# Token rows scattered to their pages in DRAM, in place of lists and row fetches

## The chip, the core and the metric

The kernel runs on one core of a Trainium2 chip. The metric is device time in microseconds (us) of one execution; the median of several runs is given. Engines are named as in the profile: PE (TensorE), with its weight loads PEld; DVE (VectorE); ACT (ScalarE); POOL (GpSimd); SP (SyncE, which here only issues DMAs and loads a register).

## What is computed

A long convolution over four sequences, gated by its own input, and then a mixture of 16 experts of which each token takes one:

```
h_filt = (maximum(pos_emb @ w1, 0) @ w2) * exp(-0.01 * pos)      # 10048 x 128
u = x * v                                                        # 4 x 10048 x 128
y = irfft(rfft(u, 2 * S) * rfft(h_filt, 2 * S))[:S]              # along the sequence
x = (x * y).reshape(40192, 128)

g_idx = argmax(x @ w_group)            # one of 4 groups, g_w its softmax weight
e_idx = argmax(x @ w_expert[g_idx])    # one of 4 experts in it, e_w its softmax weight
out[token] = g_w * e_w * (maximum(x[token] @ moe_w1[g, e], 0) @ moe_w2[g, e])   # 128 -> 1024 -> 128
```

All inputs and outputs are fp32. The expert products are made of fp32r halves: a high part (`wh`, `xh`, `hh`) and the rest (`wl`, `xl`, `hl`), three matmuls for each product.

## The kernel before

**Convolution.** The transform is a two-stage DFT. After the filter's own transform, a loop runs over b = 0..4. For b = 0..3 its first part transforms batch b: 42 parts of three channels each, whose inputs `xv` arrive by SP (L364) and are folded into even and odd halves `eo` (L380 add, L381 subtract; on POOL for batch 0 and for the first 12 parts of batches 2 and 3, on DVE otherwise), then multiplied on PE (`dft_blocks`, L320). From b = 1 on, the inverse of batch b-1 runs in the same loop: small PE transposes of `z` (`turned`, L583 and L593), `inverse_blocks` (L624), and a product with the gate `x` (L637). I call this the DFT stage of batch b. Its second part is the middle of batch b: 40 pairs of positions, each with a load `ht` (L540), two products on DVE (`t`, L551 and L554), two sums on POOL (`y`, L552 and L555) and the inverse's first product on PE. For b = 4 there is only the inverse of batch 3: the last stage.

**Routing.** A finished batch's rows `xy` are written to DRAM (`xyd`, L696). In the next middle and the DFT stage after it, the generators `chosen` and `ranked` find each token's expert, weight and place, step by step between the other work. Places are counted so that each expert's tokens fill pages of 256 rows. `ranked` then hands out 79 scatters per batch: each is one indirect DMA of POOL (L855) that writes 128 entries of 8 bytes (token number and weight) to their places in a DRAM array `list`. The program calls `scatter(3)` after each part of a DFT stage and `scatter(1)` in each pair of a middle. On POOL a scatter is held only behind the last sum `y` that was written before it (`mark`, `behind`), and the builder's scheduler places it after that.

**Experts.** 164 pages of 256 rows follow. `load_list` (L1053) loads the lists of 16 to 70 pages at once. For each page two indirect DMAs of POOL gather 2 x 128 rows of 512 bytes (`xg`, L1136, six buffers), PE transposes them (`px`, L1151), 48 matmuls make the two layers (L1189 to L1191 and L1208 to L1210), ACT scales the rows (`os`, L1229), and two indirect DMAs of POOL write them out by token (`out`, L1234, queued up to 24 pages deep). `turn` fixes the order of PE, DVE and ACT for each page over its neighbours; `fetch` sets what POOL gets in each page: two gathers first, then scatters that are still owed, then writes as far as a budget of 4.8 operations (`SHARE`) reaches. A page's second-layer weights come by SP (`ws`, L1129). Of the four differences `wl` (L1178) of a page three are made on DVE; the fourth, of the second half of `ws`, is made on POOL for pages 8 to 41 (`FROM, TO`) and on DVE for the others.

`beyond` and `between` fix POOL's order in the last part: an instruction put `between` comes after the last `beyond` before it in the program and before the next one.

Of the kernel before, what the change touches and what calls it, by code (L numbers as in the profile page):

```python
# [32 lines left out]
TP = 256  # L33
# [7 lines left out]
FROM, TO = 8, 42  # L41
XG, OS = 6, 24
SHARE = 4.8
EARLY = 16
LISTED = 3
# [9 lines left out]
NLOAD, NPROD, NSPEC, NTT, NY = 5, 5, 5, 5, 5  # L55
BIGID = 65535.0
HALVES = slice(0, 64), slice(64, 128)
# [73 lines left out]
class Kernel:  # L131
# [5 lines left out]
    def emit(self):  # L137
        tc, nc, d = self.tc, self.nc, self.d
        with ExitStack() as ctx:
# [14 lines left out]
            self.entries = ctx.enter_context(tc.tile_pool(name="entries", bufs=2))  # L154
            self.all = [Page(self, q) for q in range(pg.n)]
            self.lists = st
# [11 lines left out]
    def router_consts(self):  # L168
# [7 lines left out]
        self.keep = rp.tile([128, 8, NB], mybir.dt.bfloat16, name="keep")  # L176
# [4 lines left out]
        self.iota = rp.tile([128, 2], F32, name="iota")  # L181
# [6 lines left out]
    def conv(self, ctx, right):  # L188
# [23 lines left out]
        routing, self.scatters, self.mark = iter(()), [], None  # L212

        self.anchor, self.loose = None, []
        for b in range(self.nbat + 1):
# [13 lines left out]
            for j, (d0, n) in enumerate(groups(120, GI) + [(120, 4), (124, 4)]):  # L229
                if b > 0 and j % 2 == 0:  # L230
                    tts = self.turned(d0, min(2 * GI, D - d0))
                for i in range(2 * j, min(2 * j + 2, len(parts))):
                    self.run_ahead(b, i, made, folded)
                    self.dft_blocks(*folded[i])
                    if b > 0 and i % 2 == 0:
                        self.inverse_blocks(b - 1, xy, d0, n, tts)
                if last:
                    self.inverse_blocks(b - 1, xy, d0, n, tts)
                    next(weights, None)
                    if j == 1:  # L240
                        for p in self.all[:XG]:
                            p.gather()
# [11 lines left out]
            if not last:  # L254
                back = []
                for i, (k0, n) in enumerate(groups(NB, 2)):
# [3 lines left out]
                    final = b == self.nbat - 1  # L260
                    self.scatter(i > 3 and (i < 22 or not final))
                    if final and i == 22:
                        self.scatter(NB)
                        ready = self.load_list(0, nc.gpsimd)
                    if final and i == 26:
                        ready(nc.gpsimd)
# [13 lines left out]
    def behind(self, ins):  # L280

        if self.mark is not None:
            order = mybir.DependencyInfo(mybir.DependencyClass.NoSync, mybir.DependencyReason.DATA)
            self.tc.add_manual_dep(ins.ins, self.mark.ins.name, order, reason="in its turn")

# [4 lines left out]
    def between(self, ins):  # L290

        self.tc.keep_in_program_order(ins)
        self.after(ins, self.anchor)
# [9 lines left out]
    def scatter(self, n):  # L303
        for _ in range(n):
            if self.scatters:
                ins = self.scatters.pop(0)()
                if self.anchor is not None:
                    self.between(ins)
                else:
                    self.behind(ins)  # L310
# [35 lines left out]
    def product(self, b, d0, n):  # L346
# [3 lines left out]
        if b == 0 and d0 >= FIRST:  # L350
# [6 lines left out]
            tag, bufs = ("spec", NSPEC) if d0 // GD % 9 < 5 else ("tt", NTT)  # L357
# [12 lines left out]
    def fold(self, xt, b, d0, n):  # L370
# [8 lines left out]
        sub = nc.vector if (b or d0 >= FIRST and odd) and not early else nc.gpsimd  # L379
        self.in_turn(b, add.tensor_tensor(eo[:, :n, 0:64], lo, hi, ALU.add))  # L380
        self.in_turn(b, sub.tensor_tensor(eo[:, :n, 64:128], lo, hi, ALU.subtract))  # L381
# [31 lines left out]
    def network(self, ctx, eo):  # L413
# [6 lines left out]
        w1, w2 = tp.tile([128, 128], F32, name="w1f"), tp.tile([128, 256], F32, name="w2f")  # L420
# [40 lines left out]
    def filter(self, ctx, ahead, made, folded):  # L461
# [12 lines left out]

        ent = fp.tile([128, self.pages.nt, 2], F32, name="ent")
        nc.gpsimd.memset(ent[:, :, 0], BIGID)
        nc.gpsimd.memset(ent[:, :, 1], 0.0)
        nc.gpsimd.dma_start(d["list"].rearrange("(p t) c -> p t c", p=128), ent)
# [56 lines left out]
    def middle(self, b, k0, n):  # L535
# [19 lines left out]
        self.mark = nc.gpsimd.tensor_tensor(y[:, :n, 1], t1[:, :n, 1], t1[:, :n, 0], ALU.subtract)  # L555
# [43 lines left out]
    def inverse_blocks(self, b, xy, d0, n, tts):  # L599
# [37 lines left out]
        nc.vector.tensor_tensor(  # L637
            xy[:, :, d0 : d0 + n].rearrange("p t d -> p d t"), yt[:, :n], xo[:, :n], ALU.mult
        )

# [45 lines left out]
    def chosen(self, b, xy, oh, en):  # L686
# [6 lines left out]
        for u in range(len(units) + 2):  # L693
# [23 lines left out]
            if u > 1:  # L717
# [9 lines left out]
                if o + n == NCH or t0 + n == NB:  # L727
                    n, t0 = o + n, t0 - o
                    lg = rp.tile([128, NCH, 20], F32, tag="lg", name="lg", bufs=2)[:, :n]
# [12 lines left out]
    def ranked(self, b, oh, en):  # L742
# [55 lines left out]
        v.tensor_tensor(base, base, self.rem, ALU.subtract)  # L798
        yield
# [12 lines left out]
        for h in range(2):  # L812
# [518 lines left out]
```

## Time and profile before

| | us |
|---|---|
| median of 3 runs (lowest to highest) | 2476.6 (2474.68 to 2480.05) |
| the profiled execution's own time | 2463.86 |
| span of the profiled execution, first to last instruction | 2462.1 |
| PE busy | 2040.5 (83%) |
| DVE busy | 1744.9 (71%) |
| ACT busy | 1366.1 (55%) |
| POOL busy | 1468.6 (60%) |
| first page's `xh` to the last page's | 1238.2 to 2437.2 |

The 40 slices of the page show PE near full with three gaps, at about 500 to 570, 810 to 890 and 1090 to 1170 us. A row of a group reads: line, engine, operation, output<-input, count | busy us, mean ns of one | idle time before it and its releasers. A row of the windows gives, for a stretch of the span, each engine's busy us, and at its end the granted PE clock, the DMA engines' busy share and GB/s. A row of the timeline gives start, duration, engine, line and what was idle before it, with the releaser; "issue" is idle time in which the profile shows nothing waited for.

### The profile page before, as it was taken

The page shows a single profiled execution, that of the slowest core. Times are in us where ns is not written, and L with a number is a line of the kernel's source. Part 1 is how long each engine was busy: PE and PEld are TensorE (multiplying, and loading weights), DVE is VectorE, ACT ScalarE, POOL GpSimd, SP SyncE. Part 2 cuts the span into 40 slices and gives each one's busy share as a digit, 9 for nine tenths or more (in the row PEclk, how much of TensorE's full clock was granted, in tenths as well). Part 3 has the DMA queues.
Part 4 walks back from the last instruction along what each step waited for, and adds up shares of the span by engine and source line. Part 5 has one row for each costly group of instructions (what it writes and reads, how often), then busy time and mean ns, then how long its engine had stood idle before and what let it go on. Part 6 is the DMA issues. An engine that isn't in the chain of part 4 may idle for free. (4 is left out here: it accounts for less than half of the span.)

```text
span 2462.1 us, 53435 instructions
## 1 busy us (share of the span) xinstructions
PE 2040.5 (83%) x18062; PEld 1839.1 (75%) x18062; DVE 1744.9 (71%) x3437; ACT 1366.1 (55%) x3005; POOL 1468.6 (60%) x1490
## 2 busy tenths in 40 slices
PE   8989999836997369951989999888888898888888
PEld 8768877715886257740779999888888888888888
DVE  5787778915799247860688998677777687776776
ACT  6733544303543034320577787677676677776676
POOL 2288006871297724866067888767666667676664
PEclk9999999957998679985999999999999999998999
DMA  4899559513684137740433344333333333343332
GB/s 122 294 253 300 154 152 302 174 28 94 200 280 138 42 84 225 233 135 13 169 107 107 112 116 122 95 103 100 100 105 100 95 118 111 112 120 98 106 108 73
DMA packets 201324, 338.65 MB, mean 138 GB/s; under 512 B 38558, under 2 KB 77185, under 8 KB 201040
## 3 DMA queue, kind: packets, MB, share of 16 engines
q1 hardware_dynamic: 159824, 275.64, 37.0%
q0 software_dynamic: 31712, 43.94, 5.9%
q10 hardware_dynamic: 9504, 15.54, 2.6%
q8 instruction: 146, 2.39, 0.4%
q14 instruction: 138, 1.13, 0.1%
HBM read 282.60 MB, written 53.30 MB: 136 GB/s over the span
## 5 line engine op out<-in xcount | busy, mean ns | idle before, releaser
L1198 DVE SCALAR_TENSOR_TENSOR hl<-ph,hh 128x512 fp32r<-128x512 f32 x656 | 448.3, 687 | 241.7 <-ACT hh L1197 126.8
L1197 ACT ACTIVATE hh<-ph 128x512 fp32r<-128x512 f32 x656 | 398.0, 608 | 282.4 <-PE px L1151 92.8
L1136 POOL DMA_INDIRECT xg<-xyd,of x328 | 372.2, 1135 | 284.7 <-PE px L1151 202.1
L1234 POOL DMA_INDIRECT out<-os,to x328 | 348.4, 1062 | 123.7 <-issue 73.6
L1208 PE MATMUL py<-hh,wh 128*128 128x256 f32 x1312 | 402.9, 307 | 1.2 <-issue 1.0
L855 POOL DMA_INDIRECT list<-en,adr x316 | 332.9, 1053 | 111.8 <-issue 90.0
L1210 PE MATMUL py<-hh,wl 128*128 128x256 f32 x1312 | 376.2, 287 | 5.3 <-POOL wl L1178 5.3
L1189 PE MATMUL ph<-xh,wh 128*128 128x256 f32 x1312 | 376.5, 287 | 3.7 <-ACT wh L1171 2.6
L1191 PE MATMUL ph<-xh,wl 128*128 128x256 f32 x1312 | 376.5, 287 | 1.9 <-issue 1.6
L1190 PE MATMUL ph<-xl,wh 128*128 128x256 f32 x1312 | 376.0, 287 | 0.9 <-DVE hl L1198 0.8
L1209 PE MATMUL py<-hl,wh 128*128 128x256 f32 x1312 | 375.2, 286 | 0.9 <-issue 0.9
L552 POOL TENSOR_TENSOR y<-t 128x256 f32<-128x256 f32 (+1 forms) x160 | 118.9, 743 | 344.2 <-DVE t L551 341.8
L1210 PEld LDWEIGHTS py<-hh,wl 128*128 128x128 f32 x1312 | 254.9, 194 | 8.1 <-POOL wl L1178 8.1
L1189 PEld LDWEIGHTS ph<-xh,wh 128*128 128x128 f32 x1312 | 256.0, 195 | 4.7 <-ACT wh L1171 2.9
L1209 PEld LDWEIGHTS py<-hl,wh 128*128 128x128 f32 x1312 | 256.6, 196 | 2.6 <-issue 2.6
L1191 PEld LDWEIGHTS ph<-xh,wl 128*128 128x128 f32 x1312 | 256.0, 195 | 2.7 <-issue 0.9
L1208 PEld LDWEIGHTS py<-hh,wh 128*128 128x128 f32 x1312 | 255.8, 195 | 1.9 <-issue 1.8
L1190 PEld LDWEIGHTS ph<-xl,wh 128*128 128x128 f32 x1312 | 256.0, 195 | 0.6 <-issue 0.5
L1178 DVE TENSOR_TENSOR wl<-mw,wh 128x512 fp32r<-128x512 f32 x328 | 240.5, 733 | 0.1
L1178 DVE TENSOR_TENSOR wl<-ws,wh 128x512 fp32r<-128x512 f32 x294 | 213.3, 726 | 29.3 <-ACT wh L1171 11.6
L1171 ACT CAST wh<-ws 128x512 fp32r<-128x512 f32 x328 | 209.8, 640 | 18.9 <-PE ph L1191 11.6
L1171 ACT CAST wh<-mw 128x512 fp32r x328 | 212.6, 648 | 0.0
(228 smaller groups left out, 4285.5 us busy)
## 6 DMA issues: line engine op xcount, KB each, us to landing
ws<-m_w SPq DMA_DIRECT2D x328, 256.0 KB
ht<-hspec SPq DMA_DIRECT2D x156, 256.0 KB
xv<-xv_in SPq DMA_DIRECT2D x131, 288.0 KB
bt<-c_b SPq DMA_DIRECT2D x95, 256.0 KB
bp<-c_bp SPq DMA_DIRECT2D x76, 256.0 KB
xyd<-xy SPq DMA_DIRECT2D x57, 256.0 KB
xo<-x_out ACTq DMA_DIRECT2D x60, 237.0 KB
hspec<-hs SPq DMA_DIRECT2D x19, 512.0 KB
```

What stands on the lines that cost most here:

```text
L1136: ins = nc.gpsimd.indirect_dma_start(self.xg[:, h], None, self.src, bass.IndirectOffsetOnAxis(ap=self.of[:, h : h + 1], axis=0), bounds_ch ...
L1171: k.fix(k.nc.scalar.copy(hi, self.matrix(i, half, self.ea)))
L1178: ins = v.tensor_tensor(lo, self.matrix(i, half, self.ed), self.wh[i][half].bitcast(F32), ALU.subtract)
L1189: k.fix(nc.tensor.matmul(ph[:, j], wh, self.xh, start=True, stop=False))
L1190: k.fix(nc.tensor.matmul(ph[:, j], wh, self.xl, start=False, stop=False))
L1191: k.fix(nc.tensor.matmul(ph[:, j], wl, self.xh, start=False, stop=True))
L1197: k.fix(nc.scalar.activation(hh, ph, AF.Relu))
L1198: k.fix(nc.vector.scalar_tensor_tensor(hl, ph, 0.0, hh.bitcast(F32), ALU.max, ALU.subtract))
L1208: k.fix(nc.tensor.matmul(self.py, wh, self.hh[c], start=(c == 0), stop=False))
L1209: k.fix(nc.tensor.matmul(self.py, wh, self.hl[c], start=False, stop=False))
L1210: k.fix(nc.tensor.matmul(self.py, wl, self.hh[c], start=False, stop=(c == NC - 1)))
L1234: ins = k.nc.gpsimd.indirect_dma_start(k.d["out"], bass.IndirectOffsetOnAxis(ap=self.to[:, h : h + 1], axis=0), o[:, h], None, bounds_chec ...
```

## The change

`list`, its fill, its loads and the gathers go. A DRAM array `prow` holds the pages themselves, 256 rows of 130 floats each: the token's 128 values, its number and its weight.

- **Staging.** For each four tiles of a batch (a `Unit`; 20 per batch, 80 in all) SP loads the rows back from `xyd` into one of two buffers `stg` (L335, 256 KB), and POOL copies number and weight beside them (L336).
- **Scatters.** 79 indirect DMAs per batch write 128 rows of 520 bytes to their places in `prow` (`put`, L343). They are ordered on POOL by `between`, with the subtractions of the fold (L437, on POOL now in all 42 parts of batches 2 and 3) and the second sum `y` (L609) as their `beyond`.
- **Empty rows.** 48 plain POOL DMAs (`clear_rest`, L326, 133 KB each) write empty rows to the pages past the tokens' number in batch 1's middle; 8 indirect ones per batch (`clear`, L357) write them to the last page of each expert.
- **Pages.** A page is one plain SP load of 133 KB (L1180, three buffers). DVE copies the numbers and weights out of it (two copies of 128 x 2).
- **Beside these.** The fourth `wl` of each page from page 2 on is POOL's (L1224). Every second product with the gate in the last stage is POOL's. `ranked` works in quarters in place of halves, with some ten more small DVE instructions; `fetch` spreads the scatters that are left over the pages before they are needed; `spec` has 4 buffers in place of 5.

```
-FROM, TO = 8, 42
-XG, OS = 6, 24
+FROM = 2
+XG, OS = 3, 24
...
-NLOAD, NPROD, NSPEC, NTT, NY = 5, 5, 5, 5, 5
+NLOAD, NPROD, NSPEC, NTT, NY = 5, 5, 4, 5, 5
...
+                    self.scatter(1 + (i % 4 == 0))
                     self.dft_blocks(*folded[i])
...
-                self.scatter(3 + j % 2 * (b == self.nbat - 1))
+                if last:
+                    self.scatter(1 + j % 2)
...
+    def stage(self, k):
+        while self.staged <= min(k, len(self.units) - 1):
+            u = self.units[self.staged]
+            n = u.n
+            u.rows = self.entries.tile([128, 4, RW], F32, tag="stg", name="stg", bufs=STG)
+            src = self.d["xyd"][u.b * 128 * NB : (u.b + 1) * 128 * NB].rearrange("(p t) c -> p t c", p=128)
+            self.nc.sync.dma_start(u.rows[:, :n, 0:128], src[:, u.t0 : u.t0 + n])
+            self.beyond(self.nc.gpsimd.tensor_copy(u.rows[:, :n, 128:130], u.en[:, u.t0 : u.t0 + n]))
+            self.staged += 1
+
+    def put(self, u, t):
+        self.stage(u.k + STG - 1)
+        n = self.pages.n * TP
+        ins = self.nc.gpsimd.indirect_dma_start(
+            self.d["prow"],
+            bass.IndirectOffsetOnAxis(ap=u.adr[:, t : t + 1], axis=0),
+            u.rows[:, t - u.t0],
...
-        sub = nc.vector if (b or d0 >= FIRST and odd) and not early else nc.gpsimd
+        sub = nc.vector if (b or d0 >= FIRST and odd) and b < 2 else nc.gpsimd
-        self.in_turn(b, sub.tensor_tensor(eo[:, :n, 64:128], lo, hi, ALU.subtract))
+        ins = sub.tensor_tensor(eo[:, :n, 64:128], lo, hi, ALU.subtract)
+        self.beyond(ins) if b != "h" and b > 1 else self.in_turn(b, ins)
...
+    def load(self):
+        k, nc, pg = self.k, self.k.nc, self.k.pages
+        self.xg = k.rows.tile([128, TH, RW], F32, tag="xg", name="xg", bufs=XG)
+        src = k.d["prow"][self.q * TP : self.q * TP + TP]
+        ins = nc.sync.dma_start(self.xg, src.rearrange("(p h) c -> p h c", h=TH))
...
-        v = k.nc.gpsimd if i and half and FROM <= self.q < TO else k.nc.vector
+        v = k.nc.gpsimd if i and half and self.q >= FROM else k.nc.vector
```

POOL's order where batch 2's DFT stage ends and its middle begins, before: `eo` is the fold, `list` a scatter of batch 1's entries, `y` the middle's sums.

```order
L380 TENSOR_TENSOR eo<-xv 96x3x64
L381 TENSOR_TENSOR eo<-xv 96x3x64
L855 DMA list<-en,adr 52224x2 x60
L552 TENSOR_TENSOR y<-t_7459 128x2x128
L555 TENSOR_TENSOR y<-t_7462 128x2x128
```

The same place of POOL after: `prow` is a scatter of whole rows, `stg<-en` the copy of number and weight.

```order
L343 DMA prow<-stg,adr 52224x130
L437 TENSOR_TENSOR eo<-xv 96x3x64
L343 DMA prow<-stg,adr 52224x130
L336 COPY stg<-en 128x4x2
L343 DMA prow<-stg,adr 52224x130
L437 TENSOR_TENSOR eo<-xv 96x2x64
L343 DMA prow<-stg,adr 52224x130 x4
L606 TENSOR_TENSOR y<-t_7547 128x2x128
L609 TENSOR_TENSOR y<-t_7550 128x2x128
```

Sixty scatters in a row after the last early fold have become single ones between the folds, with four in a row at the most; the middle then has one with each pair `y`, where before it had one from its sixth pair on, for as long as any were left.

POOL's order over three pages in the first half of the experts, before: two gathers `xg`, two writes `out`, and a scatter of the last batch's entries.

```order
L855 DMA list<-en,adr 52224x2
L1234 DMA out<-os,to_15010 40448x128
L1136 DMA xg<-xyd,of_15011 128x128 x2
L855 DMA list<-en,adr 52224x2
L1234 DMA out<-os,to_15010 40448x128 x2
```

POOL over three pages after: `wl` is the difference of the second half of `ws`.

```order
L1280 DMA out<-os,to 40448x128 x2
L1224 TENSOR_TENSOR wl_25736<-ws,wh_25732 128x512
L343 DMA prow<-stg,adr 52224x130 x2
L1280 DMA out<-os,to 40448x128 x2
L1224 TENSOR_TENSOR wl_25884<-ws,wh_25880 128x512
```

A page had two gathers, one or two writes and a scatter; it has one `wl`, two writes and none to two scatters.

SP's order after over two pages: the page's load stands among the loads of `ws`, two pages ahead of its use.

```order
L1173 DMA ws<-m_w 128x512
L1180 DMA xg<-prow 128x260
L1168 TENSOR_LOAD ep
L1168 ISA x2
L1173 ISA
L1173 DMA ws<-m_w 128x512
```

SP's order after where batch 2's DFT stage ends: the staging loads `stg<-xyd` stand ahead of the loads of the next work (`xv` of the fold, `bt`, `bp` and `ht` of the middle). Each waits for the four scatters that last read its buffer.

```order
L335 DMA stg<-xyd 128x4x128
L420 DMA xv<-xv_in 96x768
L420 DMA xv<-xv_in 96x512
L599 DMA bt<-c_b 128x512 x2
L335 DMA stg<-xyd 128x4x128
L599 DMA bt<-c_b 128x512 x3
L594 DMA ht<-hspec 128x512
L335 DMA stg<-xyd 128x4x128
L600 DMA bp<-c_bp 128x512
```

Before, the same place held only `xv`, `bt`, `bp` and `ht`.

More of the change, by code (lines that the diff above doesn't have):

```diff
@@ L259, in conv @@
                         self.back(*back.pop(0))
[L260 to L266, printed above, removed]
+                    if b == 1 and i % 4 == 1:
+                        self.clear_rest(i // 4)
+                    self.scatter(NB if b == self.nbat - 1 and i == 37 else i < 37)
                     if i % 4 != 3 if i < 30 else i % 2:
@@ L292, in between @@
         self.tc.keep_in_program_order(ins)
[L293 removed]
+        if self.anchor is not None:
+            self.after(ins, self.anchor)
         self.loose.append(ins)
@@ L303, in scatter @@
     def scatter(self, n):
[L304 to L310, printed above, removed]
+        self.tick += 1
+        for _ in range(min(n, len(self.scatters))):
+            b, send, tick, u = self.scatters[0]
+            if u:
+                self.stage(u.k)
+            if tick > self.tick and n < NB:
+                break
+            self.between(send())
+            self.scatters.pop(0)
@@ new lines, in unordered, with clear_rest @@
+    def unordered(self, ins, group, *others):
+        for g in (group, *others):
+            self.tc.declare_no_dep(ins.ins, group=g, reason="every row belongs to one page and one token")
+        self.tc.add_to_no_dep_group(group, ins.ins)
+    def clear_rest(self, i):
+        q0 = self.nbat * SEQ // TP
+        qs = range(q0, self.pages.n)[i::10]
+        for q in qs:
+            dst = self.d["prow"][q * TP : q * TP + TP].rearrange("(p z) c -> p z c", z=ZR)
+            self.tc.keep_in_program_order(self.nc.gpsimd.dma_start(dst, self.empty[: TP // ZR]))
@@ L842, in ranked @@
             v.tensor_reduce(other, f.rearrange("p e t -> p t e"), AX.X, ALU.add)
[L843 to L844 removed]
+            if h:
+                v.tensor_tensor(pos, pos, other, ALU.add)
+            if h % 2:
+                yield
         v.memset(pos[64:128, NB - 1 : NB], BIGID)
         adr = self.entries.tile([128, NB], I32, tag="adr", name="adr")
[L848 to L867 removed]
+        v.tensor_copy(adr, pos)
+        for t0, n in groups(NB, 4):
+            u = Unit(b, len(self.units), t0, n, adr, en)
+            self.units.append(u)
+            self.scatters += [(b, lambda u=u, t=t: self.put(u, t), self.tick + LAGS, u) for t in range(t0, t0 + n)]
         yield
@@ L979, in work @@
             if p.xg is None:
-                p.gather()
+                p.load()
         if pages:
```

208 lines of the change are left out of this document (105 added, 103 removed).

## The prediction, made before the changed kernel was timed

> **What bounds the kernel now.** I read the page's busy shares first, then the windows cut at the stages, then inside the odd ones the waits and the timeline, and last the cadence of the pages.
>
> ```profile
> span 2462.1 us, 53435 instructions
> PE 2040.5 (83%) x18062; PEld 1839.1 (75%) x18062; DVE 1744.9 (71%) x3437; ACT 1366.1 (55%) x3005; POOL 1468.6 (60%) x1490
> ```
>
> The profiled execution took 2463.86 us, 12.7 below the median of 2476.6; I sum against it and add 12.7. PE is the fullest engine, but 422 us of the span are without it. The windows say where (the rows in order: DFT stage of batch 1, middle 1, stage 2, middle 2, stage 3, middle 3, last stage, experts).
>
> ```profile
> core 0: us, PE busy (x) PEld busy (x) DVE busy (x) ACT busy (x) POOL busy (x), PEclk, DMA share, GB/s
> 244.00:364.00 120.00, 109.73 (x1554) 95.83 (x1555) 90.68 (x184) 59.81 (x108) 2.21 (x4) 0.94 0.54 150
> 368.00:454.00 86.00, 85.00 (x555) 68.38 (x554) 73.22 (x182) 37.60 (x91) 56.98 (x78) 1.00 0.87 283
> 457.00:657.00 200.00, 132.09 (x1558) 103.84 (x1558) 103.04 (x207) 60.64 (x108) 89.39 (x86) 0.76 0.33 90
> 661.00:748.00 87.00, 85.46 (x558) 69.04 (x558) 78.59 (x185) 38.24 (x92) 77.45 (x98) 1.00 0.86 281
> 750.00:953.00 203.00, 125.65 (x1561) 104.64 (x1562) 113.15 (x230) 60.24 (x108) 96.64 (x91) 0.76 0.33 90
> 957.00:1047.00 90.00, 86.80 (x556) 69.81 (x556) 77.60 (x184) 38.18 (x91) 74.75 (x98) 0.98 0.78 256
> 1053.00:1212.00 159.00, 76.60 (x1032) 60.63 (x1029) 66.30 (x111) 36.87 (x62) 76.08 (x74) 0.73 0.28 86
> 1238.00:2438.00 1200.00, 1055.43 (x8424) 1027.33 (x8425) 927.26 (x1683) 870.88 (x1951) 848.10 (x765) 0.98 0.37 108
> ```
>
> Stages 1, 2 and 3 run the same 1550 or so matmuls. Stage 1, where POOL has four instructions, takes 120 us; stages 2 and 3, where POOL has the scatters, take 200 and 203, and the granted clock falls from 0.94 to 0.76. Three gaps hold the difference and the like in the last stage:
>
> ```profile
> 505.00:573.00 68.00, 17.68 (x55) 7.29 (x52) 3.51 (x8) 1.62 (x3) 47.80 (x48) 0.50 0.06 13
> 813.00:888.00 75.00, 15.89 (x79) 10.15 (x80) 5.85 (x14) 4.43 (x8) 51.49 (x52) 0.54 0.07 14
> 1086.00:1168.00 82.00, 10.49 (x52) 5.78 (x52) 4.51 (x6) 3.34 (x6) 58.37 (x59) 0.52 0.09 23
> ```
>
> In each, POOL does nothing but scatters and everybody else stands. DMA is at 0.06 to 0.09, so no transfer is waited for. The longest of PE's waits in the first gap, and its timeline:
>
> ```profile
> PE pt L583 <- issue: 39.3, 23, 3.1
> ```
>
> ```profile
> 548.12 0.98 POOL L855 DMA_INDIRECT list<-en,adr  x1 [0.30 <-issue]
> 548.17 0.13 PEld L583 LDWEIGHTS pt<-ident,z 128*32 128x32 f32 x1 [2.67 <-issue]
> 549.40 0.98 POOL L855 DMA_INDIRECT list<-en,adr  x1 [0.30 <-issue]
> 549.57 0.37 PE L583 MATMUL pt<-ident,z 128*32 128x128 f32 x1 [2.43 <-issue]
> ```
>
> PE waits for no semaphore, yet its next instruction comes 1.4 us after the last: weight load, matmul, weight load. POOL meanwhile sends a scatter every 1.29 us (0.98 and 0.30 of issue). So a long row of indirect DMAs on POOL goes with instructions that start slowly on PE. I don't know the mechanism; what I use is that the middles have 19 scatters each among their sums and no such gap (PE 85.46 of 87).
>
> The experts: the first row is all pages, then three stretches of them.
>
> ```profile
> L1158 ACT CAST xh<-px x164: 362/383/400, 1238.2 to 2437.2; 128x256 fp32r<-128x256 f32 x164
> L1158 ACT CAST xh<-px x15: 367/373/375, 1432.0 to 1524.2; 128x256 fp32r<-128x256 f32 x15
> L1158 ACT CAST xh<-px x21: 382/384/386, 2055.3 to 2205.3; 128x256 fp32r<-128x256 f32 x21
> L1158 ACT CAST xh<-px x4: 373/375/375, 2418.7 to 2437.2; 128x256 fp32r<-128x256 f32 x4
> ```
>
> A page takes 1199.0/163 = 7.36 us in the mean; 6.59 in 1432 to 1524, where POOL makes a `wl`; 7.50 in 2055 to 2205; and 6.17 at the end, where nothing is left to gather. What makes 7.50 of it:
>
> ```profile
> 2055.00:2205.00 150.00, 127.57 (x1042) 123.94 (x1041) 111.55 (x201) 106.74 (x241) 104.03 (x97) 1.00 0.39 113
> L1222 PE MATMUL ptm<-ident,ys 128*128 128x128 f32 x40 | 8.8, 300 | 22.4 <-ACT ys L1215 22.4
> L1234 POOL DMA_INDIRECT out<-os,to x56 | 60.2, 1074 | 17.1 <-issue 9.4 <-ACT os L1229 4.9 <-ACT wh L1171 2.7
> L1136 POOL DMA_INDIRECT xg<-xyd,of x41 | 44.9, 1096 | 30.0 <-PE px L1151 23.9 <-issue 6.1
> ```
>
> In these 20 pages the 22.4 us in front of `ptm` are all of PE's idle time (150 - 127.6), 1.12 a page, and so most of the excess (7.50 - 6.17 = 1.33). POOL has 97 indirect DMAs there, 4.85 a page, up to five in a row. ACT's copy `ys` comes late with no work ahead of it that would explain that; I read it as the small form of the same gap.
>
> **The change, part by part.** *The gaps.* The order of the change leaves no row of scatters longer than eight (the clears of batch 3) where there were about 60. Stage 2 has some 43 scatters between 42 subtractions, one in 2.8 us, thinner than the middles' 19 in their last two thirds. So I give stages 2 and 3 the 120 us of stage 1: -80 and -83. In the last stage I take PE's idle time in the gap, 82 - 10.5 = 71.5: -71.
>
> *What POOL then carries there.*
>
> ```profile
> L855 POOL DMA_INDIRECT list<-en,adr x316 | 332.9, 1053 | 111.8 <-issue 90.0 <-DVE adr L852 21.4 <-PE py L1210 0.3
> L381 POOL TENSOR_TENSOR eo<-xv 96x192 f32<-96x192 f32 x29 | 27.1, 935 | 0.0
> L637 DVE TENSOR_TENSOR z<-yt,xo 128x474 f32<-128x474 f32 (+1 forms) x22 | 21.2, 963 | 0.5
> ```
>
> A scatter of 520-byte rows isn't in the trace. Its nearest rows are the 8-byte scatter (1.05) and the 512-byte `out` (1.07, above), the dearest one the gathers of 1049 to 1068, further below. I take 1.05 + 0.30 = 1.35. Stage 2: 43 x 1.35 + 42 x 0.94 + the 12 early adds at about the same = 109 us of POOL in 120: hidden for the most part; I add 8 to each of stages 2 and 3 (bounds 0 and 20). Last stage: 33 scatters (45 us) are hidden, but eleven products go to POOL; by `wl` (1.31 on POOL, 0.68 on DVE, below) one would be 0.96 x 1.9 = 1.8 us, so 11 x 0.9 = 10 on the inverse's path, and 3 for one buffer less: +13 (0 to 25).
>
> *Middles.* POOL bounds them after the change. Middle 2: 77.45 busy + 17 more scatters x 1.35 + 10 copies `stg<-en` at about 0.4 (an estimate: 1024 elements, less than any row here) = 104 against a length of 87: +17. Middle 3 has eight clears too: 74.75 + 25 x 1.35 + 4 = 113 against 90: +23. Middle 1 gets 48 plain POOL DMAs.
>
> ```profile
> L1063 POOL DMA_DIRECT2D lst<-list x3 | 1.8, 595 | 4.0 <-DMA list<-en,adr 2.4 <-issue 1.7
> L1136 POOL DMA_INDIRECT xg<-xyd,of x12 | 16.0, 1331 | 4.4 <-issue 3.3 <-PE pbp L563 1.0
> ...
> GB/s 122 294 253 300 154 152 302 174 28 94 200 280 138 42 84 225 233 135 13 169 107 107 112 116 122 95 103 100 100 105 100 95 118 111 112 120 98 106 108 73
> ```
>
> 48 x (0.60 + 0.30) = 43 on 57 = 100 against 86: +14. Their 6.4 MB ask the same of the DMA engines: 283 GB/s x 86 us + 6.4 MB = 30.7 MB, 102 us at the 300 GB/s of the page's fullest slice (the last row).  Middles together +54; from below +20, if the `y` of one pair runs while the next scatter waits, and from above +54 + 80 x 0.28 = +76 if a scatter costs the 1.33 of the gathers in the second row. `ranked` in quarters adds small work to a DVE with 8 to 14 us to spare in each middle: 0, and 5 without that cover.
>
> *Pages.* Two gathers go from POOL (2 x 1.40 = 2.8 us), one `wl` comes (1.31) and 0.63 scatters (0.85), and two writes stay (2.74): 4.9 us a page, where 1432 to 1524 had 6.7. PE's idle time before `ptm` should go. DVE loses one `wl` and gains two small copies (about 0.13 each, as its copy `ep` below), but (timeline of that stretch, then its copies and its window):
>
> ```profile
> 1472.04 1.90 DVE L1178 TENSOR_TENSOR wl<-mw,wh 128x512 fp32r<-128x512 f32 x1
> 1472.06 1.31 POOL L1178 TENSOR_TENSOR wl<-ws,wh 128x512 fp32r<-128x512 f32 x1
> 1474.46 0.68 DVE L1178 TENSOR_TENSOR wl<-mw,wh 128x512 fp32r<-128x512 f32 x1
> ...
> L1116 DVE COPY ep<-epgi 1x1 int32<-1x1 int32 x14 | 1.3, 131 | 0.0
> ...
> 1432.00:1524.00 92.00, 89.71 (x732) 87.59 (x731) 82.75 (x138) 75.37 (x169) 77.34 (x68) 1.00 0.43 122
> ```
>
> Beside POOL's, DVE's takes 1.90 in place of 0.68: moving it off DVE saves nothing there. The stretch 1432 to 1524 (14 pages) is the template: 6.59 with that and with more POOL work than the change has. Floor 6.17. I take 6.5, near the template, since DVE, 82.75/14 = 5.9 us a page there, is near full with 0.26 more: -(7.36 - 6.5) x 163 = -140 (bounds -192 and, at 7.0, -59). The page loads (133 KB, SP) replace gathers of the same bytes: 0, by two pages of lead, some 13 us.
>
> **Sum:** -80 - 83 - 71 + 16 + 13 + 54 - 140 = -291; 2463.9 - 291 = 2173, and 12.7 for the median: **2186 us**.
>
> *A rule that speaks against this.* The Trainium skill, "SBUF — State Buffer", section "Who interferes with whom", names a single point of contention among the engines, the port pair that DVE and POOL share. By it PE's slow instructions in the gaps would not be POOL's doing, and the time would be rival C's. The rows above (a gap beside each long row of scatters, none in stage 1) speak against it here.
>
> **Rivals.** *A. The page stays heavy.* DVE's blocked `wl`, and a `wl` of POOL that stands behind a write which waits for `os`, keep it at 7.0: 2186 + 82 = 2268. For it: the template's DVE has only 0.3 us a page left. Against: the template's 6.59 with POOL at 84%.
>
> *B. The gap is a price per scatter, not per row of them.* 80 us over 60 scatters is 1.3 each; 43, 43 and 33 spread ones then cost 155, so 234 of gain become 79: 2341, and with 6.8 us pages 2390. For it: PE's rate of an instruction per 1.4 us, close to a scatter's 1.29. Against: middle 2 takes 87 with 19 scatters, middle 1 86 with none.
>
> *C. The gaps are not the scatters' doing* (something else in those stages holds PE): they stay, 2186 + 234 = 2420. Against: stage 1 has no gap, and in each of the three POOL sends scatters from end to end.
>
> *D. Slower: SP's line.* SP issues in order, and each of 80 staging loads waits for four scatters of the unit two before; behind it stand the loads of `xv` or `ht`. Four scatters last about 4 x 2.2 = 8.8 us at a middle's pace, and the cover is four buffered loads, 8.8 us as well. If each of the some 60 units of the convolution blocks longer than its cover by 291/60 = 4.9 us, all is lost; at 6 it gives 2546. Against: POOL is ordered to the same pace.
>
> That the scatters would bunch all the same is excluded by the order of the change.
>
> **How the numbers follow.** Forecast 0.48, A 0.22, B 0.12, C 0.06, D 0.10, something else 0.02. Low end: 6.17 us pages (-52), middles at +20 (-34), nothing added in the stages (-20): 2080. High end: to B's 2390, which leaves out C, D and part of B. The forecast's own range is 2080 to 2270. A measurement here tells about 0.2% from no change: faster 0.88, within 0.2% 0.02, slower 0.10.
>
> **What would show it.** Right: stages 2 and 3 in 120 to 140 us with a granted clock over 0.9; no PE wait on "issue" over 1 us between scatters; middles of 100 to 113 with POOL above 0.9 of them; a cadence of `xh` of 6.3 to 6.7 and no idle before `ptm`. Wrong: PE instructions 1.4 us apart between single scatters (B); gaps where POOL is quiet (C); `ht` or `xv` late behind `stg`, with DVE's `t` waiting for DMA (D); DVE above 0.95 of the pages and PE waiting for `hl` or `wl` (A).

## The result, and the profile after

| | before | after |
|---|---|---|
| median, us (lowest to highest, 4 runs each) | 2476.33 (2474.68 to 2480.05) | 2235.53 (2230.65 to 2243.59) |
| ratio, 95% interval | | 0.9029 [0.8996, 0.9062] |
| profiled execution's own time | 2463.86 | 2243.59 |
| span | 2462.1 | 2241.8 |
| mean granted clock | 0.926 | 0.954 |

The change made the kernel 241 us faster; 290 were forecast, and the time lies in the stated range. In the profiled executions, on which the terms were summed, the miss is larger: 220 us gained against 291 forecast. That the medians come closer is chance: the profiled execution of before lay 12.7 us under its median, that of after lies 8 over.

The page after, its busy line and the windows cut at the same stages (DFT stage 1, middle 1, stage 2, middle 2, stage 3, middle 3, the last stage in two pieces, experts). The columns are those of before.

```profile
span 2241.8 us, 54150 instructions
PE 2006.3 (89%) x18062; PEld 1824.2 (81%) x18062; DVE 1719.4 (77%) x3647; ACT 1364.4 (61%) x3005; POOL 1402.3 (63%) x1521
```

```profile
core 0: us, PE busy (x) PEld busy (x) DVE busy (x) ACT busy (x) POOL busy (x), PEclk, DMA share, GB/s
253.00:372.00 119.00, 108.46 (x1552) 95.67 (x1550) 89.88 (x181) 59.51 (x107) 1.06 (x2) 0.94 0.55 151
376.00:470.00 94.00, 87.16 (x549) 67.95 (x547) 78.87 (x189) 37.46 (x90) 77.41 (x120) 0.98 0.96 327
471.00:626.00 155.00, 125.12 (x1583) 106.08 (x1585) 109.65 (x194) 61.76 (x110) 110.47 (x130) 0.86 0.58 167
632.00:746.00 114.00, 92.74 (x557) 69.96 (x555) 80.11 (x187) 38.26 (x91) 93.75 (x121) 0.96 0.81 264
747.00:902.00 155.00, 126.78 (x1576) 107.21 (x1578) 109.83 (x221) 60.79 (x110) 104.20 (x123) 0.84 0.55 159
908.00:1030.00 122.00, 96.42 (x559) 71.92 (x559) 84.41 (x216) 39.50 (x93) 99.87 (x128) 0.94 0.67 229
1030.00:1139.00 109.00, 76.60 (x1075) 63.43 (x1076) 62.63 (x125) 38.46 (x67) 52.29 (x56) 0.88 0.55 182
1139.00:1166.00 27.00, 23.86 (x259) 15.23 (x259) 12.69 (x58) 17.46 (x52) 3.89 (x5) 0.91 0.59 216
1166.00:2211.00 1045.00, 1017.16 (x8418) 1009.42 (x8418) 897.08 (x1895) 870.89 (x1950) 715.51 (x646) 0.99 0.47 142
```

Stages 2 and 3 fell from 200 and 203 us to 155 each, though not to the 119 of stage 1, and their clock is at 0.86 and 0.84. The middles grew to 114 and 122. PE is busy for 1017 of the experts' 1045 us. The cadence of the pages, all of them and the last 55:

```profile
L1199 ACT CAST xh<-px x164: 363/375/440, 1165.7 to 2211.0; 128x256 fp32r<-128x256 f32 x164
L1199 ACT CAST xh<-px x55: 374/375/377, 1876.9 to 2211.0; 128x256 fp32r<-128x256 f32 x55
```

The groups of POOL that answer to those of before:

```profile
L343 POOL DMA_INDIRECT prow<-stg,adr x316 | 344.7, 1091 | 82.1 <-issue 47.7 <-POOL stg L336 27.4 <-DVE xv L423 1.5
L326 POOL DMA_DIRECT2D prow<-empty x47 | 25.0, 538 | 0.0
L336 POOL COPY stg<-en 128x8 f32<-128x8 f32 x80 | 21.1, 264 | 84.1 <-DMA prow<-stg,adr 70.7 <-issue 13.2
L1224 POOL TENSOR_TENSOR wl<-ws,wh 128x512 fp32r<-128x512 f32 x162 | 219.5, 1355 | 220.5 <-ACT wh L1217 216.9
```

A page takes 1045.3/163 = 6.41 us, and exactly 6.19 (334.1/54) once no scatter is left. A scatter of 520-byte rows takes 1.09 us, hardly more than one of 8-byte rows (1.05). New is the row of the copy `stg<-en`: itself 0.26 us, it waits for scatters that have not yet landed, 70.7 us in all, and what stands behind it on POOL waits too. The longest waits of stage 2:

```profile
PEld pt L647 <- ACT tt L649: 30.1, 7, 9.1
PE pt L647 <- ACT tt L649: 28.8, 7, 9.0
DVE xv L423 <- DMA xv<-xv_in: 25.0, 14, 5.6
ACT oo L686 <- DVE eo L436: 24.3, 5, 8.0
POOL stg L336 <- DMA prow<-stg,adr: 21.7, 10, 3.8
```

No wait of PE on "issue" is left among the longest: PE waits for the inverse's ACT copy `tt`, ACT stands behind `oo`, that behind DVE's fold, and that behind loads `xv` and POOL.

### The profile page after: what moved, and what is told of

It reads as the page before. It is cut to its first block, busy times and chain, and to the rows that moved or that the text cites. A ratio compares the mean times of both kernels' runs of the same rounds, so it can differ in the third digit from the quotient of the medians.

```text
span 2241.8 us, 54150 instructions
## 1 busy us (share of the span) xinstructions
PE 2006.3 (89%) x18062; PEld 1824.2 (81%) x18062; DVE 1719.4 (77%) x3647; ACT 1364.4 (61%) x3005; POOL 1402.3 (63%) x1521
## 5 line engine op out<-in xcount | busy, mean ns | idle before, releaser
L1243 ACT ACTIVATE hh<-ph 128x512 fp32r<-128x512 f32 x656 | 393.3, 605 | 130.5 <-PE ph L1237 68.7
L343 POOL DMA_INDIRECT prow<-stg,adr x316 | 344.7, 1091 | 82.1 <-issue 47.7
L1224 POOL TENSOR_TENSOR wl<-ws,wh 128x512 fp32r<-128x512 f32 x162 | 219.5, 1355 | 220.5 <-ACT wh L1217 216.9
L624 ACT COPY z<-pbp 128x512 f32<-128x512 f32 (+1 forms) x160 | 92.6, 581 | 263.3 <-PE pbp L617 225.9
L1224 DVE TENSOR_TENSOR wl<-mw,wh 128x512 fp32r<-128x512 f32 x328 | 233.5, 712 | 0.0
L447 PE MATMUL psb<-z,bt 128*128 128x256 f32 x790 | 203.6, 389 | 33.1 <-DMA bt<-c_b 15.4
```

The costliest lines, as they stand in the source:

```text
L343: ins = self.nc.gpsimd.indirect_dma_start(self.d["prow"], bass.IndirectOffsetOnAxis(ap=u.adr[:, t : t + 1], axis=0), u.rows[:, t - u.t0], ...
L1224: ins = v.tensor_tensor(lo, self.matrix(i, half, self.ed), self.wh[i][half].bitcast(F32), ALU.subtract)
L1243: k.fix(nc.scalar.activation(hh, ph, AF.Relu))
```

## The experiments

Stages, in us, of all the profiles. A DFT stage is from the first to the last matmul of `eo`, a middle from its first to its last first sum `y`, the last stage from there to the first `xh`, and a page is the mean of 163.

| | middle 0 | stage 1 | middle 1 | stage 2 | middle 2 | stage 3 | middle 3 | last | page |
|---|---|---|---|---|---|---|---|---|---|
| before | 66.9 | 119.8 | 86.5 | 200.1 | 87.0 | 202.9 | 90.3 | 191.3 | 7.36 |
| after | 71.2 | 119.6 | 93.5 | 153.8 | 113.1 | 154.4 | 121.3 | 136.5 | 6.41 |
| pace_lists | 66.7 | 118.2 | 86.5 | 129.2 | 97.9 | 139.2 | 103.6 | 148.1 | 7.64 |
| no_scatter | 66.6 | 117.5 | 86.5 | 116.1 | 86.6 | 124.2 | 86.6 | 107.0 | 6.72 |
| no_stage | 70.0 | 120.0 | 90.6 | 138.1 | 100.1 | 146.9 | 105.4 | 126.2 | 6.33 |
| stg_lag | 71.9 | 122.6 | 92.6 | 145.0 | 113.6 | 153.9 | 114.4 | 126.5 | 6.38 |
| stg_act | 70.4 | 118.2 | 92.5 | 164.6 | 112.7 | 164.3 | 114.3 | 149.5 | 6.51 |
| early_clear | 69.5 | 124.5 | 86.5 | 144.4 | 110.9 | 147.4 | 116.6 | 120.8 | 6.43 |

**pace_lists: the pacing alone.** In the kernel before:

```
-                if self.anchor is not None:
-                    self.between(ins)
-                else:
-                    self.behind(ins)
+                self.between(ins)
...
-        self.mark = nc.gpsimd.tensor_tensor(y[:, :n, 1], t1[:, :n, 1], t1[:, :n, 0], ALU.subtract)
+        self.beyond(nc.gpsimd.tensor_tensor(y[:, :n, 1], t1[:, :n, 1], t1[:, :n, 0], ALU.subtract))
...
-        sub = nc.vector if (b or d0 >= FIRST and odd) and not early else nc.gpsimd
+        sub = nc.vector if (b or d0 >= FIRST and odd) and b < 2 else nc.gpsimd
```

with `beyond` for that subtraction and the change's calls of `scatter`.

> Before, with only the pacing of the change: its 8-byte scatters stand between the fold's subtractions (all of batches 2 and 3 on POOL) and with each pair of a middle, as the rows do in the change; lists and gathers stay, and no row is staged. In the last stage the 33 scatters still stand in one row, behind 12 gathers. Theory 1 (PE is slowed by long rows of indirect DMAs, and what is left of it in the change comes from the staging): stages 2 and 3 take 120 to 130 us, middles 2 and 3 100 to 108, the last stage keeps a gap of 30 to 45 us. Theory 2 (each scatter has a price of its own, about 34/43 = 0.8 us): stages 2 and 3 take 150 or more. Theory 3 (the subtractions on POOL hold the stages): 150 too. Pages as before, 7.36 us. In all, theory 1: 140 us less less 35 for the middles, about 2360; theories 2 and 3: about 2410.

Measured: 2361.91 us, ratio 0.9592 [0.9562, 0.9622]. Windows of its stage 2 and of the row of 33 scatters that stayed in the last stage:

```profile
453.00:583.00 130.00, 112.62 (x1563) 97.00 (x1563) 103.47 (x176) 59.52 (x108) 108.54 (x104) 0.92 0.51 142
963.00:1007.00 44.00, 14.66 (x106) 7.63 (x102) 6.71 (x12) 2.23 (x4) 32.69 (x33) 0.58 0.25 72
```

Theory 1 holds: with 46 scatters spread over it, stage 2 takes 129 us, PE's waits on "issue" in it fall from 53 us to 1.8, and beside 33 in a row PE does 15 us of work in 44. Stage 3, at 139, is above the 120 to 130 expected. Lists, gathers and 8-byte entries were all still there. Pages rose to 7.64, since more scatters fell into them.

**no_stage: the rows without their staging.** Every scatter sends the constant tile `empty`, so no page has a token and no output row is written.

```
-            u.rows = self.entries.tile([128, 4, RW], F32, tag="stg", name="stg", bufs=STG)
+            u.rows = self.empty
-            self.nc.sync.dma_start(u.rows[:, :n, 0:128], src[:, u.t0 : u.t0 + n])
-            self.beyond(self.nc.gpsimd.tensor_copy(u.rows[:, :n, 128:130], u.en[:, u.t0 : u.t0 + n]))
```

> The change without its staging: no loads of the rows by SP and no copies of number and weight; all 316 scatters send 520-byte rows of one constant, empty tile, so no page has a token and nothing is written to the output. Scatters, clears and page work are all there. Theory 1: stages 2 and 3 fall from 154 to 120 to 130 us, middles 2 and 3 from 113 and 121 to 100 to 106: 80 us less in all, about 2160. Theories 2 and 3: stages stay at 150 or more, and only the middles get some 10 us each: about 2220.

Measured: 2156.38 us in one run, 87 less than the change's profiled execution and 79 less than its median (some 70 if the chip is allowed for, on which the kernel before was 0.5% faster). Theory 1 named the total (2160), but not where: stages 2 and 3 fell by 15.7 and 7.5 only (138 and 147, not 120 to 130), the middles by 13.0 and 15.9, the last stage by 10.3 and the pages by 0.08 us each, 13 us, which need not be the staging's, as these pages write nothing. So the staging is spread over everything, and the stages hold something more.

**stg_lag: staging one unit earlier.**

```
-STG = 2
+STG = 3
-            u.rows = self.entries.tile([128, 4, RW], F32, tag="stg", name="stg", bufs=STG)
+            u.rows = self.entries.tile([128, 3, RW], F32, tag="stg", name="stg", bufs=STG)
-        self.stage(u.k + STG - 1)
+        self.stage(u.k + STG - 2)
-        for t0, n in groups(NB, 4):
+        for t0, n in groups(NB, 3):
```

> The change with three staging buffers of three tiles in place of two of four, and each staged one unit ahead, into the buffer of the unit two before and not of the one just sent: copy and load then wait for scatters of 7 us ago. Theory 1, if the wait for scatters that have not landed is the staging's price: half to most of what no_stage gains, 40 to 70 us less than the change, about 2170 to 2195. If it is the traffic or the count of the loads: within 10 us of the change.

Measured: 2204.59 us, ratio 0.8944 [0.8908, 0.8980], clear of the change's interval, each against the kernel before in its own runs: 0.9% less than the change, some 21 us. The medians differ by 31 us and the profiled executions by 38; all three are under the 40 to 70 expected. The wait of POOL's copy for scatters is gone from its waits. Middle 2 did not move (113.6). There SP stands before its staging loads until scatters have landed, and DVE waits for `ht`, which SP issues behind them (without staging, in no_stage's middle 2, 5.3 us):

```profile
SPq L335 <- DMA prow<-stg,adr: 43.5, 10, 6.1
DVE t L605 <- DMA ht<-hspec: 15.4, 8, 4.4
```

**stg_act: the staging loads on ACT's queue.** In stg_lag:

```
-            self.nc.sync.dma_start(u.rows[:, :n, 0:128], src[:, u.t0 : u.t0 + n])
+            self.nc.scalar.dma_start(u.rows[:, :n, 0:128], src[:, u.t0 : u.t0 + n])
```

> As stg_lag, with the staging loads issued by ACT's queue and not by SP's. If what is left of the staging's price (stages 145 and 154 against 138 and 147 without staging, middles 114 against 100 and 105) is xv, ht and bt waiting behind staging loads in SP's order: 20 to 35 us less than stg_lag. If it is the traffic (256 KB a unit beside loads that run near 300 GB/s in the middles): within 10 us of stg_lag, or slower by what ACT then waits.

Measured: 2271.89 us, ratio 0.9199 [0.9165, 0.9233]. The total is 67 us over stg_lag, so the 20 to 35 us that SP's order was to be worth were not won. The middles stay (112.7 and 114.3), but what is waited for in them changes. DVE's wait for `ht` is no longer among middle 2's waits, though the same bytes move in the same time: in stg_lag `ht` was late by SP's order, not by the traffic. In its place ACT's copies `z` stand behind the staging loads, which now wait for scatters on ACT's queue:

```profile
ACT z L624 <- DMA prow<-stg,adr: 21.9, 4, 7.4
```

The stages got worse by 20 and 10 us; in stage 2 ACT's copies wait 16.4 us in this way. The bytes were not varied by themselves.

**no_scatter: what a spread scatter costs.** pace_lists without its scatters; all list entries stay empty, so each page gathers one row and writes nothing.

```
-        self.scatters += [lambda t=t: put(t) for t in range(NB)]
```

> The paced lists with all 316 scatters of entries left out: every entry of the list stays empty, each page gathers one and the same row and writes nothing, and the work of the pages is otherwise all there. The subtractions of batches 2 and 3 are still on POOL. It splits what the paced stages 2 and 3 (129 and 139 us) have over stage 1 (118 to 120). If single scatters have a price of their own: 118 to 122 in both. If the subtractions on POOL, or the routing that runs there, hold them: 129 and 139 stay. Middles 2 and 3, paced 98 and 104: 85 to 88 if the scatters on POOL are all of it. Last stage, without any row: about 107 to 115.

Measured: 2106.28 us in one run. Stages 2 and 3 take 116.1 and 124.2, middles 86.6 both. In stage 2 the subtractions on POOL cost nothing. The scatters do: 13.1 us for 46 in stage 2, 0.3 each, and 15.0 in stage 3; 11.3 and 17.0 in the middles.

**plain_row: the same rows of plain DMAs.** Entries go to consecutive places, so tokens land on pages of other experts.

```
-            ins = nc.gpsimd.indirect_dma_start(
-                d["list"],
...
+            q = (b * NB + t) * 128
+            ins = nc.gpsimd.dma_start(d["list"][q : q + 128], en[:, t, :])
```

> Before, with each indirect scatter of entries replaced by a plain POOL DMA of the same 128 x 8 bytes to consecutive places, so tokens land on pages of other experts. POOL still has rows of them (33, 31 and 64 long). If any long row of POOL DMAs slows PE: the last stage keeps its gap, some 64 x 0.9 = 58 us long, PE starting an instruction every 1.4 us or less often. If it takes indirect ones: PE runs on beside the row, stages 2 and 3 take 120 to 130 us and the last stage 110 to 125.

Measured: 2224.83 us in one run. The last stage takes 116.6 us in place of 191.3, and PE works on beside the DMAs. The window of most of it, and then the group:

```profile
960.00:1041.00 81.00, 71.01 (x1030) 59.44 (x1031) 62.76 (x109) 37.54 (x63) 48.11 (x75) 0.96 0.77 171
```

```profile
L856 POOL DMA_DIRECT2D list<-en x316 | 175.5, 559 | 60.3 <-DMA list<-en 55.0 <-issue 4.8
```

It takes indirect DMAs to slow PE so, or rows without a pause: the plain ones waited for earlier ones again and again, and the longest piece without a wait was 9 DMAs (4.9 us), so this run doesn't tell the two apart. Stages 2 and 3 missed the expectation, at 148.2 and 146.4. It is not the gap, since no wait of PE on "issue" in stage 2 is over 0.4 us; what it is was not followed.

**wl_pool: less per page, gathers kept.** In the kernel before:

```
-FROM, TO = 8, 42
+FROM, TO = 2, 1000
```

> Before, with the fourth wl of every page from page 2 on made on POOL, lists and gathers as they were. By its budget POOL then has 3.8 indirect DMAs a page in place of 4.85. If the number of indirect DMAs in a page is what delays ys: 6.6 us a page as in pages 28 to 42, about 120 us less than before. If it is the gathers as such: 7.2 or more a page, within 30 us of before.

Measured: 2476.42 us in one run. Neither expectation fits: the total is within 30 us of before, as the second had it, but a page takes 7.15 us in the mean and the pages are of two kinds. Its pages in two stretches, and PE's longest wait in the second (1645 to 1990):

```profile
L1158 ACT CAST xh<-px x55: 372/373/423, 2004.2 to 2365.1; 128x256 fp32r<-128x256 f32 x55
L1158 ACT CAST xh<-px x41: 365/373/377, 1644.7 to 1990.6; 128x256 fp32r<-128x256 f32 x41
```

```profile
PEld py L1210 <- POOL wl L1178: 75.8, 38, 4.0
```

The first is the template as forecast, 361/54 = 6.68 us. In the second, where writes had piled up and scatters were due, POOL has 1.3 for `wl` and about 5.5 indirect DMAs a page, more than a page lasts, and PE waits for `wl`: 8.65 us. Behind the last page's `xh` stand 78 us, 25 in the kernel before, in which POOL sends 51 writes that were left over. With the gathers kept, POOL couldn't carry `wl` in every page.

**wl_dve: the fourth `wl` back on DVE.** In the change:

```
-FROM = 2
+FROM = 100000
```

> The change with the fourth wl of every page on DVE. The prediction says that DVE gets nothing from moving it to POOL, since its own wl waits 1.2 us for POOL's: then a page takes 6.3 to 6.5 us as in the change (6.41), the whole within 20 us of it. If the move is what makes the page light: 6.7 or more, 50 us or more slower than the change.

Measured: 2326.45 us, ratio 0.9422 [0.9392, 0.9452], some 4% slower than the change, against my expectation. Yet its last 60 pages:

```profile
L1199 ACT CAST xh<-px x60: 373/375/377, 1930.2 to 2295.2; 128x256 fp32r<-128x256 f32 x60
```

The window of a row of 13, and a piece of its timeline:

```profile
1526.00:1538.00 12.00, 4.53 (x19) 3.49 (x18) 1.29 (x2) 1.33 (x3) 7.85 (x8) 0.66 0.73 244
```

```profile
1528.83 0.98 POOL L357 DMA_INDIRECT prow<-empty,fidx  x1 [0.30 <-issue]
1529.18 0.28 PE L1255 MATMUL py<-hl,wh 128*128 128x256 f32 x1 [0.44 <-issue]
1529.90 0.29 PEld L1256 LDWEIGHTS py<-hh,wl 128*128 128x128 f32 x1 [1.24 <-issue]
1530.12 0.98 POOL L1280 DMA_INDIRECT out<-os,to  x1 [0.30 <-issue]
```

Those take 365.0/59 = 6.19 us each with all of `wl` on DVE: as work it is indifferent, as I had said. The earlier pages are slow because `wl` was the one `beyond` that POOL met in each page. Without it scatters and writes form rows of 6 to 13, and PE's instructions start slowly again: 4.5 us of work in 12 beside such a row.

**spacer: a copy of one element in `wl`'s place**, so that POOL still meets each page's `wh`.

```
-        v = k.nc.gpsimd if i and half and self.q >= FROM else k.nc.vector
...
+        if i and half and self.q >= FROM:
+            one = k.sp.tile([128, 1], F32, tag="one", name="one", bufs=2)
+            k.beyond(k.nc.gpsimd.tensor_copy(one, self.wh[i][half][:, 0:1].bitcast(F32)))
+        ins = k.nc.vector.tensor_tensor(lo, self.matrix(i, half, self.ed), self.wh[i][half].bitcast(F32), ALU.subtract)
```

> The change with the fourth wl of every page on DVE, as in wl_dve, and in POOL's place for it a copy of one element of wh by 128 partitions, which waits for the same wh and is a `beyond` like it. Theory (POOL's wl matters only as the thing that breaks POOL's rows of scatters and writes once a page; as work it is indifferent): no rows of six, pages of 6.3 to 6.45 us as in the change, in all within 20 us of it, some 80 to 90 us less than wl_dve. Rival (DVE without that wl is what makes the pages light): pages of 6.8 or more, as wl_dve, about 2320.

Measured: 2259.77 us, ratio 0.9176 [0.9151, 0.9202]; profiled span 2247.5 against the change's 2241.8; pages (2218.2 - 1161.4)/163 = 6.48. No row of six is left. Most of the 4% is back with no real work on POOL, so the theory holds in the main. Its sizes missed: pages came out 0.03 over the range, the median is 24 us over the change's and 67 under wl_dve's, and the ratio is still 1.6% above the change's. PE's waits on "issue" in the pages are 14 us here, 33 in wl_dve and 0.2 in the change.

**early_clear: stg_lag with the clears moved.** The 47 plain DMAs of empty rows (I had counted 48) go to stage 1, where four of them are sent twice, and in middle 3 only scatters of older batches are flushed.

```
-                    if b == 1 and i % 4 == 1:
-                        self.clear_rest(i // 4)
-                    self.scatter(NB if b == self.nbat - 1 and i == 37 else i < 37)
+                    old = sum(1 for s in self.scatters if s[0] < b - 1)
+                    self.scatter(old if b == self.nbat - 1 and i == 37 else i < 37)
```

> stg_lag with the 48 plain DMAs of empty rows in stage 1, where POOL is idle, in place of middle 1, and without the flush that puts batch 2's eight clears in front of the middle's last sums in middle 3: these clears come singly in the last stage. Expected: middle 1 back from 93 to 87 us, stage 1 unchanged (120), the PE gap of 15 us at the end of middle 3 gone and some of it (0 to 5) back in the last stage: 15 to 20 us less than stg_lag. If the clears cost the same wherever they stand: no change from stg_lag.

It answers to these lines of the change at the end of middle 3, where eight clears stand ahead of the last sum `y`:

```profile
1030.20 1.05 POOL L357 DMA_INDIRECT prow<-empty,fidx  x1 [0.17 <-issue]
...
1040.14 1.12 POOL L357 DMA_INDIRECT prow<-empty,fidx  x1 [0.30 <-issue]
1041.28 0.74 POOL L609 TENSOR_TENSOR y<-t 128x256 f32<-128x256 f32 x1
...
1042.08 1.22 PE L617 MATMUL pbp<-y,bp 128*128 128x256 f32 x2 [15.17 <-POOL y L609]
```

Measured: 2201.7 us, ratio 0.8946 [0.8916, 0.8976]: no change from stg_lag that can be measured. Middle 1 fell to 86.5 and the gap of 15 us is gone, but stage 1 rose by 2 and the pages by 0.05 us each, 8 in all; the profiled execution is 10 us shorter, and the medians do not show it. Inconclusive.

**row_fill and spec4, on another chip.** The results name the chip: 12, 11 and 4 for the ten experiments so far, 2 for these two; for the runs of the change itself none is named. Both edits are to the kernel before, first row_fill's:

```
                     self.behind(ins)
+                    if self.last is not None:
+                        self.after(ins, self.last)
+                    for _ in range(6):
+                        self.last, old = self.nc.gpsimd.memset(self.fill, 0.0), self.last if _ else ins
+                        self.tc.keep_in_program_order(self.last)
+                        self.after(self.last, old)
```

and spec4's:

```
-NLOAD, NPROD, NSPEC, NTT, NY = 5, 5, 5, 5, 5
+NLOAD, NPROD, NSPEC, NTT, NY = 5, 5, 4, 5, 5
-            tag, bufs = ("spec", NSPEC) if d0 // GD % 9 < 5 else ("tt", NTT)
+            tag, bufs = ("spec", NSPEC) if d0 // GD % 9 < 4 else ("tt", NTT)
```

> Before, with six memsets of 128 x 24 on POOL (about 0.1 us each) behind each scatter of entries up to the last stage, so that the rows of 60 and 63 scatters keep their places but have one indirect DMA per 1.7 to 2.0 us in place of 1.29. If PE is slowed by indirect DMAs that follow each other without a pause: PE goes on at its usual pace beside them, its instructions are not 1.4 us apart, and stage 2 is bound by POOL, 60 x 1.9 us = 114 us after the row's start at about 488: some 150 us in place of 200. If each scatter costs PE the same wherever it stands: the gap is as deep and longer, stage 2 takes 220 us or more.

> Before, with four buffers of spec in place of five. The change's middle 0, which has no scatter and no staging, takes 71 us in place of 67. If the buffer is the cause: middle 0 takes 70 to 72 us here and the others 0 to 4 us more; if not (other waits of the change's start): 67.

Measured: row_fill 2268.36 us, spec4 2123.62, one run each, and the kernel before beside them, one run, **2110.71 us** where the other chips gave 2458 to 2486. spec4's trace shows why. The windows of its stage 2, of the inside of its row of 60 scatters, of its last stage and of its pages, and then a piece of that row:

```profile
462.00:592.00 130.00, 112.31 (x1562) 98.03 (x1562) 104.27 (x209) 61.02 (x109) 94.58 (x87) 0.92 0.53 141
510.00:577.00 67.00, 60.41 (x876) 53.07 (x872) 50.47 (x102) 30.43 (x54) 52.38 (x49) 0.95 0.54 138
917.00:1022.00 105.00, 94.63 (x1340) 75.40 (x1339) 85.26 (x199) 59.24 (x121) 73.68 (x69) 1.00 0.58 186
1022.00:2097.00 1075.00, 1021.35 (x8418) 1012.52 (x8419) 920.86 (x1682) 864.70 (x1949) 850.43 (x773) 0.98 0.40 120
```

```profile
539.96 0.98 POOL L855 DMA_INDIRECT list<-en,adr  x1 [0.30 <-issue]
540.90 1.00 PE L583 MATMUL pt<-ident,z 128*32 128x128 f32 x24
541.24 0.98 POOL L855 DMA_INDIRECT list<-en,adr  x1 [0.30 <-issue]
```

The same scatters follow each other every 1.28 us, and PE runs 24 of its `pt` transposes in the time of one: 60 of 67 us busy, where before had 17.7 of 68. Pages take 6.59 us in the mean with all their gathers, and half of them at most 6.19, where the median of the kernel before was 7.67; one row of gathers and writes there is 264 long, with no pause over 0.6 us. PE's idle time in front of `ptm`, in the kernel before and then in spec4:

```profile
L1222 PE MATMUL ptm<-ident,ys 128*128 128x128 f32 x322 | 68.9, 296 | 131.9 <-ACT ys L1215 126.2 <-ACT hh L1197 2.4 <-DVE tot L762 1.3
L1222 PE MATMUL ptm<-ident,ys 128*128 128x128 f32 x322 | 62.7, 277 | 22.7 <-ACT ys L1215 22.5 <-ACT hh L1197 0.2
```

So the late `ys` of the pages goes with the gaps of the stages. Here a row of indirect DMAs doesn't slow PE. So row_fill can't answer its question on this chip; its POOL rows only grew longer and held up middles 2 and 3, which began 65 and 80 us after the last matmul of the stage before them, where 4 had been usual. spec4's middle 0 took 72.8 us, row_fill's 66.9 with five buffers: the buffer is worth 6 us, a little over what was expected.

## Why the prediction was right, and where its sizes were off

| term | forecast | measured in the profiles |
|---|---|---|
| stage 2, stage 3 | -72, -75 | -46.3, -48.5 |
| last stage | -58 | -54.8 |
| middles 1, 2, 3 | +14, +17, +23 | +7.0, +26.1, +31.0 |
| pages | -140 | -153.7 |
| ahead of stage 1; behind the last page's `xh` | 0, 0 | +8.1, +5.9 |
| between the stages | 0 | +4.9 |
| sum | -291 | -220.3 |

**The gaps: right.** Long rows of indirect DMAs were the cause on the chips where the gap was seen. pace_lists moved the scatters, and the subtractions to POOL, which cost nothing in stage 2; the gaps of stages 2 and 3 went; the row that it left kept its gap; wl_dve brought rows back and with them slow instructions. Rival C fell with that.

**Stages 2 and 3: mis-sized by 26 us each.** The step that failed is "hidden for the most part; I add 8". pace_lists and no_scatter show 13.1 and 15.0 us for the spread scatters, so each keeps a price of 0.3 to 0.4 us: rival B was wrong by its 1.3 but right that there is one. no_stage against pace_lists gives 9 and 8 for the rest of the change beside the staging (wider rows, clears, `ranked` in quarters; not told apart). The staging has the other 15.7 and 7.5. I had taken the staging loads for a matter of rival D alone and given them nothing in the sum. Stage 1 was also not quite the right yardstick: without scatters stage 3 takes 124, not 120.

**Last stage: near, and in part by luck.** Without any scatter it takes 107.0 us (no_scatter), 84 less than before where I took 71. The staging gives back 10, and eight clears hold PE for 15 us and not for their own 11 (1030.2 to 1041.3), since they stand ahead of a sum `y` that PE waits for; I had put them into middle 3. The products on POOL took 1.26 us each and not 1.8.

**Middles: mechanism half right.** POOL's part of the sum holds: paced or without staging, middles 2 and 3 take 98 to 105 us (forecast 104, and 113 with the clears or 102 without), with POOL busy for 0.92 and 0.93 of them in no_stage. The staging adds 13 and 16, which I had left out, and with it POOL is busy for only 0.82: it does not bound them alone. Middle 1's clears took 0.54 us each and not 0.90, and are 47.

**Pages: right, a little better than forecast.** 6.41 where I took 6.5, with the floor of 6.17 (6.19) confirmed over 54 pages. That DVE would gain nothing from the moved `wl` was right. spec4's pages bear out the reading of the late `ys` as a small form of the gap: in the change PE waits 11.7 us for it in all the pages, where the kernel before had 126.2. But what the `wl` does on POOL I had missed: it keeps scatters and writes apart, and that is worth more than its place on either engine (wl_dve, spacer). Rival A did not happen.

**Rival D: its mechanism is there, at a smaller price.** In stages 2 and 3 of the change DVE waits 25.0 and 31.0 us for `xv`, against 10.4 and 17.2 without staging, and in stg_lag's middle 2 `ht` is late behind SP's staging loads. The staging costs 70 to 87 us in all (no_stage), not the 291 from which D would decide. 21 to 38 us of it go when the copy and the load no longer wait for scatters that have just been sent (stg_lag, which eases POOL's wait and SP's together).

**The signs.** Of those named for "right" the cadence came, and no wait of PE on "issue" is over 0.4 us in stage 2. The stages at 154 us with a clock of 0.86 and 0.84, middle 3 at 121 and POOL at 0.82 of the middles did not come, and D's sign, `xv` late, came in part. So the time lies in the range with the gaps and the pages explained rightly and the staging not foreseen. A slip in the low end: "nothing added in the stages" is -16, or -29 with the last stage, and not -20.

**Not foreseen:** 4 us of the 8 ahead of stage 1 lie in middle 0, and they are `spec`'s fifth buffer (spec4). What stands behind the last page, and between the stages, was not followed.

**The rule weighed there** (the Trainium skill, "SBUF — State Buffer", "Who interferes with whom") would have left the gaps where they were; on the chips that showed them pace_lists decides against it. No run here shows through what PE is held.

**What stays open** is larger than these terms: on the chip of the last two runs the kernel before took 2110.71 us, less than the change took on the others, because rows of scatters did no harm there. The change was not run on that chip. If the staging costs the same there (70 to 87 us here), the change would have little left to win it back with; whether it is slower there was not tried.

## What to carry to other kernels

When an engine shows time before its instructions that nothing in the profile accounts for, look at what the others do back to back just then, and break that up before making it cheaper: 8-byte scatters between other work of POOL gave 4% with not one of them saved, on a chip that showed the gap. In order to pace one engine, hang its work on something that waits for the consumer once in each step; a copy of one element does it. A copy into a buffer that was sent a moment ago is a wait in the middle of an in-order queue, and one buffer more, filled one step earlier, removes it.

## What the runs showed of the hardware that was not expected

- PE's slowness depends on how many indirect DMAs of POOL follow each other. In pace_lists' row of 33, PE did 15 us of work in 44; with single ones between other work, each cost about 0.3 us (13.1 us for 46); rows of 6 to 13 are enough to be seen in the pages. Plain DMAs of POOL, 0.56 us each, did not do it in pieces of up to 9.
- It is not a property of the kernel alone: one chip ran the same rows, at the same 0.98 us a scatter, without any slowing, and the same kernel in 2110.71 us in place of 2458 to 2486. In its pages PE waited 22.5 us for `ys` in place of 126.2. One run of it, and the traces of two variants, are all there is from that chip.
- A scatter of 128 rows costs POOL nearly the same for 8 bytes a row (1.05 us) and for 520 (1.09).
